# Attention and MLP-mixer kernel: keys in three chunks of 128 rows and a block-diagonal remainder, one score group a pair, PSUM tiles of two banks

## Chip, cores, metric

One core of one Trainium2 chip. The metric is the device time of one execution in microseconds (us), slowest (here: only) core, median of several runs. The kernel before takes 408.87 us (406.52 to 409.55).

The kernels of each comparison ran on the same chip as the kernel before. All medians below are of such runs. Different experiments ran on different chips, so across experiments the ratios compare better than the medians. A ratio is the mean time of one kernel's fast runs over the mean of the kernel before's fast runs of the same rounds, so it is not quite the ratio of the medians beside it. Times inside a profile are from the start of the profiled span.

## The reference

```python
# q, k, v: (8 batches, 12 heads, 448 rows, 64), tau = 0.1
q_n = q / (norm(q) + 1e-6);  k_n = k / (norm(k) + 1e-6)
attn = softmax(q_n @ k_n^T / tau)                    # per head
x    = (attn @ v) with heads side by side            # (8, 448, 768)
h    = relu(x^T @ w_tok1) @ w_tok2                   # over the 448 rows, 256 wide
u    = x + h^T
out  = u + relu(u @ w_ch1) @ w_ch2                   # over 768 columns, 1536 wide
```

## The kernel before

It works on pairs of heads: 6 pairs a batch, 48 in all. For a pair: load q, k, v (sync queue); square and sum them; scale q and k by their norms on POOL (`kq`); transpose (`qk`, by PE at first, by a DMA transpose from pair 12 on); scores on PE (`psS`), exp on ACT (`pt`), P times V (`psO`), divide (`x`), the two token matmuls (`psR`, `rt`, `psU`), the sum `u`, and a DMA transpose of `u` (`ut`), which the channel MLP (`psG`, `psF`) reads when all six pairs of the batch are there. MLP units (one `psG` or `psF` of six or twelve matmuls) are fed between the steps of later pairs, so that PE need not wait.

```python
# 4 chunks of SC = 112 rows; ps: 4 one-bank PSUM tiles, ps2: 2 two-bank tiles
def load_v(i):                                    # load_qk is the same for q and k
    ...
    nc.sync.dma_start(out=pipe[i]["v"][:].rearrange("p g c e -> p g (c e)"),
                      in_=v[b, h0:h0 + 2].rearrange("g (p c) e -> p g (c e)", c=NCH))
def tpose_dma(i):                                 # needs kq of pair i, from POOL
    ...
    nc.sync.dma_start_transpose(out=st["qk"]..., in_=st["kqn"]...)
def tok2(i, pe=False):
    ...                                           # psU, then u = psU + x
    nc.sync.dma_start_transpose(out=ut[b][:, pj], in_=u.rearrange("p m d -> p (m d)"))

for i in ...:                                     # one pair; cut to its order
    if pj == 0 and b >= 2:
        queue += ch2_units(b - 2)
    score(i, 0); score(i, 1)
    sums(i + 4); ...; squares(i + 5)
    feed(quota * 0.22)
    pv(i - 1, 0); pv(i - 1, 1)
    scaled(i + 2); tpose_dma(i + 2)
    cast_v(i); load_v(i + 4)
    feed(quota * 0.28, least)
    score(i, 2); score(i, 3)
    feed(quota * 0.25, least)
    tok1(i - 1)
    feed(quota * 0.25, least)
    tok2(i - 1)                                   # same pair as tok1
    if pj == 0:
        queue += ch1_units(b - 1)                 # behind ch2 units that are still queued
```

Of the kernel before, what the change touches and what calls it, by code (L numbers as in the profile page):

```python
# [7 lines left out]
FP32 = mybir.dt.float32  # L8
# [14 lines left out]
def kernel(  # L23
# [35 lines left out]

    MAIN = [(128 * m, 128 * (m + 1)) for m in range(3)]  # L60
# [21 lines left out]
    ps = ctx.enter_context(tc.tile_pool(name="ps", bufs=4, space=bass.MemoryType.PSUM))  # L82
    ps2 = ctx.enter_context(tc.tile_pool(name="ps2", bufs=2, space=bass.MemoryType.PSUM))
# [10 lines left out]

    def load_qk(i):
        b, h0 = i // NPAIR, 2 * (i % NPAIR)
        if i // HP not in half:
            n = i // HP
            half[n] = dict(ssq=nrm.tile([SC, 2, 6 * NCH], FP32, name=f"ssq_{n}", tag="ssq"),
                           rn=nrm.tile([SC, 2, 6 * NCH], FP32, name=f"rn_{n}", tag="rn"))  # L100
        st = pipe[i] = {}
        for nm, src in (("q", q), ("k", k)):
            st[nm] = qkv.tile([SC, 2, NCH, E], FP32, name=f"{nm}f_{i}", tag=f"{nm}f")
            nc.sync.dma_start(out=st[nm][:].rearrange("p g c e -> p g (c e)"),
                              in_=src[b, h0:h0 + 2].rearrange("g (p c) e -> p g (c e)", c=NCH))

    def load_v(i):
        b, h0 = i // NPAIR, 2 * (i % NPAIR)
        pipe[i]["v"] = qkv.tile([SC, 2, NCH, E], FP32, name=f"vf_{i}", tag="vf", bufs=4)
        nc.sync.dma_start(out=pipe[i]["v"][:].rearrange("p g c e -> p g (c e)"),  # L110
                          in_=v[b, h0:h0 + 2].rearrange("g (p c) e -> p g (c e)", c=NCH))
# [6 lines left out]
    tiny = cst.tile([SC, 1], FP32, name="tiny")  # L118
    nc.gpsimd.memset(tiny[:], 1e-18)
    eps = cst.tile([SC, 1], FP32, name="eps")  # L120
# [10 lines left out]
    for i in range(NV):  # L131
        vt = cst.tile([SC, 6, NCH, E + 2], FP16, name=f"vt{i}")
        nc.gpsimd.memset(vt[:, :, :, E:E + 2].rearrange("p g c e -> p (g c) e"), 1.0)
        vts.append(vt)
    pts = []
    for i in range(2):
        pt = cst.tile([SC, 8 * S + 64], FP16, name=f"pt{i}")
        nc.gpsimd.memset(pt[:, 8 * S:8 * S + 64], 0.0)
        pts.append(pt)
    nc.gpsimd.memset(w1t[64:128, 3, :], 0.0)  # L140
# [33 lines left out]
    def cast_v(i, eng=None):  # L174
        g = 2 * (i % HP)
        (eng or nc.gpsimd).tensor_copy(
            out=vts[(i // HP) % NV][:, g:g + 2, :, 0:E].rearrange("p g c e -> p (g c) e"),
            in_=pipe[i]["v"][:].rearrange("p g c e -> p (g c) e"))

    def square(i, a, act=False):  # L180
        if "sq" not in pipe[i]:
            pipe[i]["sq"] = nrm.tile([SC, 2, 2 * NCH, E], FP32, name=f"sq_{i}", tag="sq")
        src = side(i, a).rearrange("p g c e -> p (g c) e")
        if act:
            nc.scalar.activation(out=pipe[i]["sq"][:, a], in_=src, func=AF.Square)  # L185
        else:
            nc.gpsimd.tensor_mul(out=pipe[i]["sq"][:, a], in0=src, in1=src)  # L187

    def side(i, a):
        return pipe[i]["kq"[a]][:]  # L190
# [5 lines left out]
    def sums(i, a0=0, a1=2):  # L196
        lo = 2 * NCH * (i % HP)
        nc.vector.tensor_reduce(out=half[i // HP]["ssq"][:, a0:a1, lo:lo + 2 * NCH],  # L198
                                in_=pipe[i]["sq"][:, a0:a1], axis=AXX.X, op=ALU.add)

    def norms(i0, i1, a0=0, a1=2, dve=False, act=False):
        n = i0 // HP
        sl = slice(2 * NCH * (i0 - HP * n), 2 * NCH * (i1 - HP * n))
        ssq, rn = half[n]["ssq"][:, a0:a1, sl], half[n]["rn"][:, a0:a1, sl]
# [10 lines left out]
    def scale(i, a, eng=None):  # L215
        st = pipe[i]
        if "kqn" not in st:
            st["kqn"] = att.tile([SC, 2, NCH, 2, E], FP16, name=f"kq_{i}", tag="kq")
        lo = 2 * NCH * (i % HP)
        rn = half[i // HP]["rn"][:, a, lo:lo + 2 * NCH].rearrange("p (g c) -> p g c", g=2)  # L220
        (eng or nc.gpsimd).tensor_tensor(out=st["kqn"][:, a].rearrange("p c g e -> p g c e"), in0=side(i, a),  # L221
                                         in1=_bcast_free(rn, E), op=ALU.mult)
# [5 lines left out]
    def tpose(i, a0=0, a1=2):  # L228
        st = pipe[i]
        if "qk" not in st:  # L230
            st["qk"] = att.tile([128, 2, NCH, SC], FP16, name=f"qk_{i}", tag="qk")
        pst = ps.tile([128, a1 - a0, NCH, SC], FP16, name=f"pst_{i}_{a0}", tag="b")
        for a in range(a0, a1):
            for c in range(NCH):
                nc.tensor.transpose(pst[:, a - a0, c, :], st["kqn"][:, a, c].rearrange("p g e -> p (g e)"),  # L235
                                    id16[:SC, :SC])
        nc.vector.tensor_copy(out=st["qk"][:, a0:a1], in_=pst[:])

    def tpose_dma(i):
        st = pipe[i]  # L240
        st["qk"] = att.tile([128, 2, NCH, SC], FP16, name=f"qk_{i}", tag="qk")
        nc.sync.dma_start_transpose(out=st["qk"][:].rearrange("p a c s -> p (a c) s"),
                                    in_=st["kqn"][:].rearrange("p a c g e -> p (a c g e)"))

    def warm(n):
        if "warm" not in pipe:
            pipe["warm"] = ps.tile([128, 128], FP32, name="warm", tag="b")
        for _ in range(n):
            nc.tensor.matmul(pipe["warm"][:], id16[:], id16[:], start=True, stop=True)

    def score(i, c):
        qk = pipe[i]["qk"][:].rearrange("p a c s -> p (a c s)")
        psS = ps2.tile([128, 2, 512], FP32, name=f"psS_{i}_{c}", tag="s")
        for hh in range(2):
            hb = hh * 64
            nc.tensor.matmul(psS[:, hh, 0:S], qk[hb:hb + 64, c * SC:c * SC + 128],  # L256
                             qk[hb:hb + 64, S:2 * S], start=True, stop=True)
        nc.scalar.activation(out=pts[i % 2][:, 2 * S * c:2 * S * (c + 1)].rearrange("p (h s) -> p h s", h=2),  # L258
                             in_=psS[0:SC, :, 0:S], func=AF.Exp, scale=inv_tau)

    def pv(i, hh):
        st = pipe[i]
        b = i // NPAIR
        if hh == 0:
            st["x"] = att.tile([128, 4, 128], FP16, name=f"x_{i}", tag="x", bufs=3)
        vt = vts[(i // HP) % NV]
        g = 2 * (i % HP) + hh
        psO = ps.tile([128, 4, E + 2], FP32, name=f"psO_{i}_{hh}", tag="b")
        for m, lo in enumerate(windows(b)):
            for c in range(NCH):  # L270
                at = (2 * c + hh) * S + lo
                nc.tensor.matmul(psO[:, m, 0:E + 1], pts[i % 2][:, at:at + 128],  # L272
                                 vt[:, g, c, 0:E + 1], start=(c == 0), stop=(c == NCH - 1))
# [5 lines left out]
    def tok1(i):  # L279
        st = pipe[i]  # L280
        w1 = (0, 1, 2, 3) if (i // NPAIR) % 2 == 0 else (4, 0, 1, 2)
        psR = ps.tile([128, TT, 128], FP32, name=f"psR_{i}", tag="b")
# [7 lines left out]
    def tok2(i, pe=False):  # L290
# [5 lines left out]
        psU = ps.tile([128, 4, 128], FP32, name=f"psU_{i}", tag="b")  # L296
# [17 lines left out]
    def m_ch1(b, ct):  # L314
# [4 lines left out]
        psG = ps.tile([128, S], FP32, name=f"psG_{b}_{ct}", tag="b")  # L319
        for dt in range(DT):  # L320
            nc.tensor.matmul(psG[:], wc1t[:, dt, ct * 128:(ct + 1) * 128],  # L321
# [275 lines left out]
```

## Time and profile before

| | before |
|---|---|
| profiled span, mean clock | 406.0 us, 0.982 |
| first score of pair 7 / 12 / 14 / 47 | 50.0 / 80.5 / 98.7 / 343.6 us |
| pairs 14 to 47 (33 pairs) | 244.9 us, with 372 `psG` and 444 `psF` matmuls |
| from pair 47's first score to the end | 62.4 us |

I split the span like this throughout: the start up to pair 14, the steady part, and the end.

```profile
143.44 1.20 SPq L305 DMA_TRANSPOSE ut<-u  x1
144.69 0.58 SPq L104 DMA_DIRECT2D qf<-in_q_dram  x1
145.32 0.45 SPq L104 DMA_DIRECT2D kf<-in_k_dram  x1
145.88 1.22 SPq L242 DMA_TRANSPOSE qk<-kq  x1
147.20 0.59 SPq L110 DMA_DIRECT2D vf<-in_v_dram  x1
```

There are five issues a pair. The `ut` transpose stands where `u` has just been made, with nothing in front of it that waits for POOL.

### The profile page before, as it was taken

The page shows a single profiled execution, that of the slowest core. Times are in us where ns is not written, and L with a number is a line of the kernel's source. Part 1 is how long each engine was busy: PE and PEld are TensorE (multiplying, and loading weights), DVE is VectorE, ACT ScalarE, POOL GpSimd, SP SyncE. Part 2 cuts the span into 40 slices and gives each one's busy share as a digit, 9 for nine tenths or more (in the row PEclk, how much of TensorE's full clock was granted, in tenths as well). Part 3 has the DMA queues.
Part 4 walks back from the last instruction along what each step waited for, and adds up shares of the span by engine and source line. Part 5 has one row for each costly group of instructions (what it writes and reads, how often), then busy time and mean ns, then how long its engine had stood idle before and what let it go on. Part 6 is the DMA issues. An engine that isn't in the chain of part 4 may idle for free.

```text
span 406.0 us, 10118 instructions
## 1 busy us (share of the span) xinstructions
PE 389.1 (96%) x4146; PEld 240.4 (59%) x4146; DVE 206.4 (51%) x441; ACT 240.8 (59%) x392; POOL 218.5 (54%) x257
## 2 busy tenths in 40 slices
PE   6978799999999999999999999999999999999995
PEld 5656566566555665656656655556655666655562
DVE  5767877655454466554555555635636345312031
ACT  5857789954676438773587437773588535521400
POOL 7797999948557480949175852949092800000000
PEclk9868999999999999999999999999999999999999
DMA  8999999978859786867759697978974433103022
GB/s 198 239 175 251 246 262 230 209 195 180 201 142 191 140 200 157 197 161 171 201 127 187 156 184 188 164 152 187 195 130 94 114 81 92 28 15 116 2 74 81
DMA packets 102590, 64.07 MB, mean 158 GB/s; under 512 B 61328, under 2 KB 98960, under 8 KB 102544
## 3 DMA queue, kind: packets, MB, share of 16 engines
q1 hardware_dynamic: 96928, 58.22, 64.0%
q0 software_dynamic: 5616, 5.21, 8.1%
q8 instruction: 32, 0.52, 0.6%
q14 instruction: 14, 0.11, 0.1%
HBM read 43.45 MB, written 11.01 MB: 134 GB/s over the span
## 4 chain that ended last, share of the span: by engine, by line
PE 87%; DMA 5%; DVE 4%; POOL 1%; issue 1%; ACT 1%; SPq 0%; DVEq 0%; POOLq 0%
PE psF L336 27%; PE psG L321 27%; PE psO L272 12%; PE psS L256 10%; PE psU L299 5%; PE psR L285 5%; DMA kf<-in_k_dram 4%; DVE ssq L198 2%; DMA qf<-in_q_dram 1%; DVE x L276 1%; PE pst L235 1%; POOL kq L221 0%; ACT sq L185 0%; DVE ost L340 0%; DVE rt L288 0%
## 5 line engine op out<-in xcount | busy, mean ns | idle before, releaser
L258 ACT ACTIVATE pt<-psS 112x896 f16<-112x896 f32 x192 | 166.2, 914 | 84.4 <-PE psS L256 84.1
L321 PE MATMUL psG<-ut,wc1t 128*128 128x448 f16 x576 | 122.4, 353 | 0.0
L336 PE MATMUL psF<-wc2t,gt 128*128 128x384 f16 x672 | 116.6, 326 | 0.0
L221 POOL TENSOR_TENSOR kq<-kf,rn 112x512 f16<-112x512 f32 x47 | 50.0, 1063 | 99.3 <-ACT rn L213 86.3
L336 PEld LDWEIGHTS <-gt 128*128 128x128 f16 x672 | 63.1, 98 | 43.4 <-issue 5.2
L340 DVE TENSOR_TENSOR ost<-psF,u 128x384 f32<-128x384 f32 (+1 forms) x64 | 35.7, 557 | 96.2 <-PE psF L336 96.0
L324 ACT ACTIVATE gt<-psG 128x448 f16<-128x448 f32 x96 | 52.3, 545 | 53.7 <-PE psG L321 53.5
L321 PEld LDWEIGHTS <-wc1t 128*128 128x128 f16 x576 | 51.3, 98 | 46.6 <-issue 8.2
L198 DVE TENSOR_REDUCE ssq<-sq 112x16 f32<-112x1024 f32 (+1 forms) x49 | 58.1, 1189 | 9.0 <-ACT sq L185 6.4
L272 PEld LDWEIGHTS <-pt 112*128 112x128 f16 x1536 | 53.5, 99 | 15.5 <-ACT gt L324 7.0
L256 PE MATMUL psS<-qk 64*128 64x448 f16 x384 | 56.2, 363 | 3.5 <-ACT pt L258 2.7
L272 PE MATMUL psO<-vt,pt 112*128 112x65 f16 x1536 | 59.3, 195 | 0.1
L302 DVE TENSOR_TENSOR u<-psU,x 128x512 f16<-128x512 f32 x48 | 33.1, 689 | 34.2 <-PE psU L299 34.2
L187 POOL TENSOR_TENSOR sq<-kf 112x512 f32<-112x512 f32 x46 | 47.7, 1037 | 3.9 <-DMA kf<-in_k_dram 3.4
L221 POOL TENSOR_TENSOR kq<-qf,rn 112x512 f16<-112x512 f32 x45 | 46.8, 1041 | 0.0
L288 DVE TENSOR_SCALAR rt<-psR 128x256 f16<-128x256 f32 x48 | 20.2, 421 | 46.8 <-PE psR L285 46.6
L276 DVE TENSOR_TENSOR x<-psO,rec 128x256 f16<-128x256 f32 x96 | 40.8, 425 | 3.3
L187 POOL TENSOR_TENSOR sq<-qf 112x512 f32<-112x512 f32 x39 | 40.5, 1037 | 0.0
L285 PE MATMUL psR<-x,w1t 128*128 128x128 f16 x384 | 29.8, 221 | 2.6 <-DVE x L276 2.6
L285 PEld LDWEIGHTS <-w1t 128*128 128x128 f16 x384 | 25.0, 99 | 11.6 <-issue 3.3
L299 PEld LDWEIGHTS <-w2t 128*128 128x128 f16 x384 | 25.9, 100 | 9.0 <-issue 2.1
L299 PE MATMUL psU<-rt,w2t 128*128 128x128 f16 x384 | 30.1, 223 | 0.4 <-DVE rt L288 0.2
(40 smaller groups left out, 156.0 us busy)
## 6 DMA issues: line engine op xcount, KB each, us to landing
qf<-in_q_dram SPq DMA_DIRECT2D x48, 224.0 KB, 3.8
kf<-in_k_dram SPq DMA_DIRECT2D x48, 224.0 KB, 3.7
vf<-in_v_dram SPq DMA_DIRECT2D x48, 224.0 KB, 3.7
out_dram<-ost SPq DMA_DIRECT2D x8, 336.0 KB, 3.1
wc1t<-in_moe_w_ch_dram POOLq DMA_DIRECT2D x4, 576.0 KB, 8.2
wc2t<-in_moe_w_ch_dram POOLq DMA_DIRECT2D x2, 1152.0 KB, 16.3
out_dram<-ost SPq DMA_DIRECT2D x8, 288.0 KB, 2.9
out_dram<-ost SPq DMA_DIRECT2D x8, 240.0 KB, 2.8
```

Of the source, the lines that this page charges most:

```text
L187: nc.gpsimd.tensor_mul(out=pipe[i]["sq"][:, a], in0=src, in1=src)
L198: nc.vector.tensor_reduce(out=half[i // HP]["ssq"][:, a0:a1, lo:lo + 2 * NCH], in_=pipe[i]["sq"][:, a0:a1], axis=AXX.X, op=ALU.add)
L221: (eng or nc.gpsimd).tensor_tensor(out=st["kqn"][:, a].rearrange("p c g e -> p g c e"), in0=side(i, a), in1=_bcast_free(rn, E), op=ALU.mult)
L256: nc.tensor.matmul(psS[:, hh, 0:S], qk[hb:hb + 64, c * SC:c * SC + 128], qk[hb:hb + 64, S:2 * S], start=True, stop=True)
L258: nc.scalar.activation(out=pts[i % 2][:, 2 * S * c:2 * S * (c + 1)].rearrange("p (h s) -> p h s", h=2), in_=psS[0:SC, :, 0:S], func=AF.Exp ...
L272: nc.tensor.matmul(psO[:, m, 0:E + 1], pts[i % 2][:, at:at + 128], vt[:, g, c, 0:E + 1], start=(c == 0), stop=(c == NCH - 1))
L276: nc.vector.tensor_tensor(out=st["x"][:, :, hh * E:(hh + 1) * E], in0=psO[:, :, 0:E], in1=_bcast_free(rec[:], E), op=ALU.mult)
L285: nc.tensor.matmul(psR[:, tt], w1t[:, w1[m], tt * 128:(tt + 1) * 128], st["x"][:, m], start=(m == 0), stop=(m == 3))
L299: nc.tensor.matmul(psU[:, m], w2t[:, tt, lo:lo + 128], st["rt"][:, tt], start=(tt == 0), stop=(tt == TT - 1))
L321: nc.tensor.matmul(psG[:], wc1t[:, dt, ct * 128:(ct + 1) * 128], ut[b][:, dt].rearrange("p m s -> p (m s)")[:, lo:lo + S], start=(dt == 0) ...
L324: nc.scalar.activation(out=gt[:, ct, (b % 2) * S:(b % 2 + 1) * S], in_=psG[:], func=AF.Relu)
L336: nc.tensor.matmul(psF[:], gt[:, ct, lo:lo + 128], wc2t[:, ct, dh * DH:(dh + 1) * DH], start=(ct == 0), stop=(ct == CT - 1))
```

## The change

Its intent: fewer switches of PE's tiling mode, fewer and fuller score matmuls. The keys of a head come in three chunks of 128 rows. The last 64 keys of both heads share a fourth chunk, with block-diagonal zeros, so that one 128-row matmul scores both heads (`score_rest`). Their P times V part runs directly behind the score group in the same 64-row mode (`pv_rest`). PSUM becomes three two-bank and two one-bank tiles. The core of the diff (cut: tile shapes, memsets, the first six pairs, weight padding, MLP functions that only gain a `wide` argument):

```diff
-    ps = ...(tc.tile_pool(name="ps", bufs=4, ...))
-    ps2 = ...(tc.tile_pool(name="ps2", bufs=2, ...))
+    ps = ...(tc.tile_pool(name="ps", bufs=2, ...))
+    ps2 = ...(tc.tile_pool(name="ps2", bufs=3, ...))
+    def load_rows(t, src):                       # for k and v
+        nc.sync.dma_start(out=t[:, 0:2 * KC]..., in_=src[:, 0:128 * KC]...)
+        nc.sync.dma_start(out=t[:, 2 * KC], in_=src[:, 128 * KC:S])
     def scale(i, a, eng=None):
+        ...                                      # 3 chunks of k in one instruction, and
+        if a == 0:
+            for g in range(2):
+                p = slice(64 * g, 64 * g + 64)
+                (eng or nc.gpsimd).tensor_scalar_mul(out=kq[p, 0, KC, g], in0=src[p, 2 * KC], scalar1=rn[p, 2 * KC:KS])
+    def score_rest(i):
+        psQ = ps2.tile([128, 512], FP32, ...)
+        nc.tensor.matmul(psQ[:, 0:S], qk[:, 0, KC], qk[:, 1, :, 0:SC], start=True, stop=True)
+        nc.scalar.activation(out=pts[i % 3][...], in_=psQ[:, 0:S], func=AF.Exp, scale=inv_tau)
+    def pv_rest(i):                              # 8 matmuls of 64 rows, two banks in turn
+        ...
+    def refill(b, n):
+        while queue:
+            unit()
+        queue.extend(ch1_units(b) + ch2_units(b))
+        fed[:] = [0.0, sum(t for t, _ in queue) / n]
-    (the order of the kernel before, above)
+    for i in range(NPAIR + 1, NP_ALL):
+        for c in range(KC):
+            score(i, c)
+        pv_rest(i - 1); pv(i - 1, 0); pv(i - 1, 1)
+        if pj == 2 and b > 1:
+            refill(b - 1, 6)                     # batch b-1's MLP starts at once
+        side(i)                                  # load_qk, sums, squares, scaled,
+                                                 # tpose_dma(i + 2), cast_v(i), load_v(i + 4)
+        unit(True)
+        score_rest(i)
+        tok2(i - 2)                              # a pair later than tok1(i - 2)
+        ...                                      # units that are due
+        tok1(i - 1)
```

## The prediction

> **What bounds the kernel now.** I read the page first, busy times and slices:
>
> ```profile
> PE 389.1 (96%) x4146; PEld 240.4 (59%) x4146; DVE 206.4 (51%) x441; ACT 240.8 (59%) x392; POOL 218.5 (54%) x257
> ...
> PE   6978799999999999999999999999999999999995
> ...
> PEclk9868999999999999999999999999999999999999
> DMA  8999999978859786867759697978974433103022
> ```
>
> PE is full from slice 6 (about 52 us) to the end, at full clock; only the first eighth has PE gaps and a reduced clock (6 in slice 3). The DMA row is highest in just that part (8 and 9). The chain that ended last agrees: PE 87%, DMA 5%. Next, how full PE is when it is full, by stretches (us, PE, PEld, DVE, ACT, POOL busy, clock, DMA share, GB/s):
>
> ```profile
> 20.00:30.00 10.00, 7.60 (x92) 5.64 (x90) 6.79 (x13) 6.34 (x11) 9.80 (x12) 0.64 1.02 174
> ...
> 80.00:320.00 240.00, 239.89 (x2630) 144.91 (x2629) 125.61 (x266) 152.29 (x238) 145.74 (x161) 1.00 0.76 167
> ```
>
> From 80 to 320 us no other engine is over 64%, so there time is the sum of PE's work. The same stretch holds 1056 matmuls of psO, 32 a pair of heads: 33 pairs, 240/33 = 7.27 us a pair. "PE busy" says nothing of how well it is used, so I read the timeline of one pair (start, length of what is merged):
>
> ```profile
> 201.94 0.55 PE L256 MATMUL psS<-qk 64*128 64x448 f16 x4
> 202.42 1.19 PE L272 MATMUL psO<-vt,pt 112*128 112x65 f16 x32
> 203.45 1.30 PE L321 MATMUL psG<-ut,wc1t 128*128 128x448 f16 x6
> 204.68 0.55 PE L256 MATMUL psS<-qk 64*128 64x448 f16 x4
> ```
>
> Starts, not lengths, add up here. Six psG matmuls take 6 x 0.189 = 1.13 us (starts inside a group are 0.189 us apart; 448 columns take 0.187 at the 2.4 GHz of the clock-gate page named below), so psG's share ends at 204.58, psS starts 0.10 later, and the next psG at 205.16. A score group of four thus takes 0.58 us. In the instruction records its matmuls start 3 ns apart in pairs and the pairs 0.20 apart: the two heads' 64-row matmuls run side by side. Two pairs need 0.374 us of columns; 0.207 is lost on entering and leaving. All 79 groups between 52 and 340 us show it (median 0.581). psO: 203.45 - 202.42 = 1.03 us for 32 matmuls, 32 ns each.
>
> **What the Trainium skill says.** "TensorEngine Tiling (Array Packing)", Key Properties: going from one tiling mode to another drains the array. The trace agrees and gives the size, 0.10 us in and 0.10 us out. "TensorE: Matmul & The Clock Gate", Part 3, The mechanism: matmuls on different row groups overlap, some 4 ns apart; here 3 ns. The same page, Part 1: after an idle window the clock is halved until work has been dense again; the 0.64 in 20 to 30 us agrees. "DMA: Bandwidth & Descriptors", Why a DMA increments its semaphore by 16 and not by 1 (How many engines): a transfer runs on the largest number up to 16 that divides the slowest dimension of both sides. All loads before have 112 partitions outside, so 16; nothing in this trace shows a smaller number.
>
> **The change, part by part.**
>
> *PE, score.* Before, a pair has two groups of two side-by-side pairs: 2 x 0.581 = 1.162 us. After, one group of three (3 x 0.19 + 0.207 = 0.78) and one 128-row matmul for both heads' last 64 keys (0.189, no mode change because of block-diagonal zeros): 0.97. Columns are the same (4 x 448 either way); what is saved is one entry and exit, 0.2 us.
>
> *PE, P times V.* Before 32 x 32 ns = 1.03 us. After 24 x 32 ns = 0.77 and eight 64-row matmuls that sit directly behind the score group, in its mode, alternating row halves and PSUM banks. If each two run side by side as the scores do: 4 x about 0.035 = 0.14 (estimate); if not, 8 x 32 ns and nothing is saved. Saving 0.11, or 0.
>
> Together 0.31 us a pair (0.2 without overlap). Pairs 7 to 47 run where PE is full: 41 x 0.31 = 12.7 us (8.4). The other matmuls do not change.
>
> *ACT.* Four exps of 896 columns at 914 ns = 3.66 us a pair become three and one of 448. The relu of 128x448 has a row, 545 ns, so 3.29 us: 0.37 less. That is beside PE's work in the full stretch and worth something only before 52 us, where `psS` waits for `pt` (2.7 us in five waits): up to 7 x 0.37 = 2.6 us.
>
> *POOL.* The k scaling shrinks from 512 to 384 columns (1063 to about 800 ns) but gains two 64-column pieces of about 0.2 us; the k square and v cast shrink by an eighth (0.13, 0.08 us). Even, and POOL is at 61%. *DVE:* the reduction has 960 columns for 1024 (1210 to about 1135 ns); eleven memsets at the start fit before its first work at 4.4 us.
>
> *PSUM and order.* psO and what else is narrow now share two banks, where four served. `pv_rest` needs both, directly after the scores, and one was just filled by psR, whose relu takes 421 ns on DVE. The score group lasts 0.78 us, so this mostly fits, but when DVE is inside a reduction PE waits: I allow 0.07 us a pair, 3 us. Third two-bank tile: scores no longer wait for two exps. tok2 now follows a whole pair later, so its waits on `rt` stay away.
>
> *DMA.* q loads stay: 224 packets of 1024 B. k and v become 256 packets of 768 B and 128 of 256 B, and three more matters follow. The transposes go from 112 to 128 rows (896 to 1024 packets each). In the packet records 1024 B takes a median 46 ns, 256 B 18, 3072 B 121, so 768 B should take about 37 (interpolated). Spread over 16 engines a pair costs 42 x 46 = 1.93 us of each engine before, and 14 x 46 + 32 x 37 + 16 x 18 = 2.12 after: +10%, harmless. But the small load has two heads outside on the DRAM side and 128 partitions on the other, and by the rule above it runs on two engines: 64 packets each. For those two the pair costs 14 x 46 + 32 x 37 + 128 x 18 = 4.13 us, twice as much. With transposes (64 + 32 packets, 1.73), stores (0.57) and the rest they are busy about 6.6 us of a pair of 7.0: only just under the bound. Before 52 us the pairs follow every 4.6 us (first `psS` after a wait at 34.25, then 38.85) and the weights pass too, so there these two engines are over it. Loads up to k of pair 10 and v of pair 7 need 11 x 2.41 + 8 x 1.77 = 41 us there, with weights and transposes (about 11 us by the same packet times) 52 us, against the 50 us at which pair 7 starts now. I expect the start to lengthen by 5 to 9 us if the rule holds (I give it two chances in three), 2 us if not; against it stand the exps' 2.6 us and about 1 us from the extra warming matmuls, which keep the clock from the 0.64.
>
> Sum: 408.9 - 12.7 (PE) + 3 (PSUM waits) + 2 (start: 0.67 x 7 + 0.33 x 2 - 3.6 = 1.7) + 1 (later waits for two full DMA engines, a third of a possible 3) = about 402 us.
>
> **Rivals.**
> 1. *The PE saving arrives whole and the small loads spread or hide.* For: the full stretch has no engine over 64%, loads run seven pairs ahead, mean DMA share is 0.76 with peaks above. Then 409 - 12.7 - 2 + 2 = 396, or 393 if no PSUM wait appears.
> 2. *Two DMA engines become the bound.* For: the share of 0.76 to 1.2 is already high, the chain before 60 us holds waits for kf and qf, and 6.6 of 7.0 us leaves no room for HBM packets of 256 B slower than the 18 ns, which I know only from transposes inside SBUF. At 25 ns it is 7.5 us a pair: 41 x (7.5 - 6.96) = +22 us on rival 1, about 418. Against: a schedule this tuned would hardly keep it.
> 3. *The PV remainder does not overlap,* or its weight loads do not: 4 us less gain, about 406.
> 4. *PSUM with two narrow banks stalls PE.* At 0.3 us a pair all is given back: 409. Against: between the users of one bank lies at least one MLP unit of 1.13 us, longer than any evacuation (reciprocal and multiply 0.6, u 0.69).
>
> **Range and chances.** The PE term is the firmest (8 to 14 us off); the DMA terms can cost nothing or 20 us. 391 covers rival 1 with full overlap and a better start; 416 covers rival 2 at its milder end. The 2% line, 400.7 us, lies just under the point, so faster and same are about even; slower needs rival 2.
>
> **What would show it.** Right: score matmuls in groups of six, 0.58 for two groups gone; per pair 7.0 us between 80 and 320; remainder matmuls 3 ns apart in pairs; small loads landing later than large ones; pair 7 starting at 50 to 57 us. Wrong: PE idle or half clock after 80 us with the releaser DMA or POOL (rival 2), psO waiting for DVE `rt` (rival 4), remainder starts 32 ns apart (rival 3), or a start shorter than 48 us.

## More of the kernel before

The loads of q, k and v, the stores and the DMA transposes are issued by one engine, SP, in program order (the weights by POOL). The rows with SPq are the sync queue's timeline in the steady part (start, length of the issue, what is issued).

The group rows of POOL, the engine that prepares k and q (count, busy us and mean ns of one, then idle time before them):

```profile
L221 POOL TENSOR_TENSOR kq<-kf,rn 112x512 f16<-112x512 f32 x47 | 50.0, 1063 | 99.3 <-ACT rn L213 86.3
L187 POOL TENSOR_TENSOR sq<-kf 112x512 f32<-112x512 f32 x46 | 47.7, 1037 | 3.9 <-DMA kf<-in_k_dram 3.4
```

From 49 to 83 us POOL has hardly a gap, and waits for k loads take only 3.4 us in all.

## The result

The changed kernel takes 453.54 us (453.34 to 453.63, four runs), the kernel before 409.21 (406.52 to 410.17) in the same rounds: ratio 1.109, 95% interval 1.104 to 1.115. It is slower by 44 us and far outside the range of 391 to 416. The page of the changed kernel, parts 1, 2 and 4:

```profile
PE 395.9 (88%) x4120; PEld 255.8 (57%) x4120; DVE 212.5 (47%) x454; ACT 224.3 (50%) x392; POOL 243.7 (54%) x352
...
PE   6878599779599996999699997999599997999995
PEclk9889779989799998999889998999899996999999
...
PE 67%; DMA 8%; DVE 8%; POOL 7%; ACT 4%; issue 3%; SPq 1%; POOLq 0%; ACTq 0%
```

The PE row is no longer a row of nines. From slice 8 on it falls to 5, 6 or 7 every few slices, down to the end, and the clock row falls to 6, 7 or 8 about there. The chain holds PE for 67% and not 87%; DMA, DVE and POOL have 8, 8 and 7%.

| us | before | changed |
|---|---|---|
| start, to pair 14 | 98.7 | 113.5 |
| pairs 14 to 47 | 244.9 | 284.3 |
| rest | 62.4 | 54.1 |
| span | 406.0 | 451.9 |

The rest is shorter because the changed kernel has done more of the MLP by pair 47 (426 `psG` and 432 `psF` matmuls between 14 and 47, against 372 and 444). At 0.19 and 0.163 us each that is 54 x 0.19 - 12 x 0.163 = 8.3 us. For the same work the steady part is thus 284.3 - 8.3 - 244.9 = 31 us longer. The start is 14.8 us longer; it holds 12 `psF` matmuls more (72 against 60), so for the same work 14.8 - 12 x 0.163 = 12.8.

**PE's work did get shorter.** One pair of the changed kernel on PE, to hold against the four lines of before in the prediction:

```profile
106.86 0.74 PE L275 MATMUL psS<-qk 64*128 64x448 f16 x6
107.44 0.30 PE L295 MATMUL psO<-vt,pt 64*128 64x65 f16 x8
107.67 0.92 PE L304 MATMUL psO<-vt,pt 128*128 128x65 f16 x24
108.43 2.11 PE L368 MATMUL psF<-wc2t,gt 128*128 128x384 f16 x12
110.38 0.35 PE L282 MATMUL psQ<-qk 128*128 128x448 f16 x1
110.57 0.61 PE L331 MATMUL psU<-rt,w2t 128*128 128x128 f16 x8
```

By starts: six score matmuls 0.58 us, the eight remainder matmuls 0.23 (with one mode switch), P times V 0.76, the 128-row score 0.19 (110.57 - 110.38). With about 0.1 to enter the mode (as before) that is 1.86 us, against 2 x 0.58 + 1.03 = 2.19 before. The overlap is there: 0.23 less the switch of 0.10 leaves 0.13 us for eight matmuls, not 8 x 0.032. In the instruction records the eight start within 92 to 111 ns in every pair from 14 to 46, where 32 ns apart would take 224; 72 of the 132 couples start less than 10 ns apart, as the prediction had asked for.

**Where PE stands instead.** Two waits of PE that the kernel before does not have (us in total, times, longest):

```profile
PE psG L353 <- DMA ut<-u: 21.3, 6, 4.5
PE psO L295 <- POOL vt L198: 11.8, 10, 4.0
```

and the sync queue's waits for POOL and for `u` in the changed kernel, then the one for POOL before:

```profile
SPq L262 <- POOL vt L198: 46.1, 10, 9.5
SPq L337 <- DVE u L334: 27.0, 8, 6.6
```
```profile
SPq L242 <- POOL vt L176: 31.6, 15, 3.4
```

Six times, once a batch, the first `psG` of a batch waits for the last `ut`. SP waits 46 us for POOL in front of the `qk` transposes. It waited there before too, but shorter at a time and with no `ut` transpose behind it that was urgent. The timeline around the first of the six, all engines, lines left out:

```profile
111.22 0.69 DVE L334 TENSOR_TENSOR u<-psU,x 128x512 f16<-128x512 f32 x1
...
112.64 0.54 SPq L113 DMA_DIRECT2D qf<-in_q_dram  x1
...
113.79 1.04 POOL L236 TENSOR_TENSOR kq<-qf,rn 112x512 f16<-112x512 f32 x1
...
114.86 1.76 SPq L262 DMA_TRANSPOSE qk<-kq  x1
...
116.37 1.11 PE L353 MATMUL psG<-ut,wc1t 128*128 128x448 f16 x5
116.72 0.52 SPq L101 DMA_DIRECT2D vf<-in_v_dram  x1
117.96 2.04 SPq L337 DMA_TRANSPOSE ut<-u  x1
...
121.95 0.53 PE L353 MATMUL psG<-ut,wc1t 128*128 128x448 f16 x1 [4.47 <-DMA ut<-u]
122.28 0.58 PE L282 MATMUL psQ<-qk 128*128 128x448 f16 x1
122.65 1.06 PE L331 MATMUL psU<-rt,w2t 128*128 128x128 f16 x8
```

`u` is done at 111.91. Its transpose is issued at 117.96, because the queue in front of it holds the pair's loads, the `qk` transpose (which waits until POOL has scaled q, 113.79 plus 1.04) and the v loads. `psG` has started at 116.37 with the five pairs that are there, needs the sixth, and PE stands for 4.47 us. After that PE runs at half clock: the next matmul of 448 columns takes 0.37 us to its successor and not 0.19, eight `psU` matmuls take 1.06 and not 0.61. The records show the same doubled spacing after each of the six stalls.

Two things of the change make this. The instruction records of the last pair of each batch (six batches, the first and the last left out) show both, in us:

| | `u` done to its transpose issued | `u` done to the first `psG` of the batch |
|---|---|---|
| before | 0.0 to 0.4 | 12.2 to 28.4 |
| changed | 4.9 to 6.1 | 3.9 to 4.5 |

Before, ch1 units joined the queue behind ch2 units, so a transpose had at least 12 us. Now `refill` starts them at once, and `tok2`, a pair later and behind `side`, gets its place in the queue last.

### The profile page after: what moved, and what is told of

Its sections match the earlier page's. It is cut to its first block, busy times and chain, and to the rows that moved or that the text cites. A ratio compares the mean times of both kernels' runs of the same rounds, so it can differ in the third digit from the quotient of the medians.

```text
span 451.9 us, 10222 instructions
## 1 busy us (share of the span) xinstructions
PE 395.9 (88%) x4120; PEld 255.8 (57%) x4120; DVE 212.5 (47%) x454; ACT 224.3 (50%) x392; POOL 243.7 (54%) x352
## 4 chain that ended last, share of the span: by engine, by line
PE 67%; DMA 8%; DVE 8%; POOL 7%; ACT 4%; issue 3%; SPq 1%; POOLq 0%; ACTq 0%
PE psG L353 22%; PE psF L368 20%; PE psO L304 7%; PE psS L275 6%; PE psU L331 5%; DMA ut<-u 5%; DMA kf<-in_k_dram 4%; PE psR L317 3%; POOL kq L236 3%; DVE ssq L215 3%; DVE x L308 2%; POOL kq L243 2%; PE psO L295 2%; PE psQ L282 2%; POOL sq L208 1%
## 5 line engine op out<-in xcount | busy, mean ns | idle before, releaser
L276 ACT ACTIVATE pt<-psS 128x896 f16<-128x896 f32 x144 | 122.3, 917 | 71.1 <-PE psS L275 71.1
L353 PE MATMUL psG<-ut,wc1t 128*128 128x448 f16 x576 | 127.5, 372 | 21.5 <-DMA ut<-u 21.3
L236 POOL TENSOR_TENSOR kq<-kf,rn 128x384 f16<-128x384 f32 x47 | 39.9, 849 | 106.7 <-ACT rn L229 105.9
L353 PEld LDWEIGHTS <-wc1t 128*128 128x128 f16 x576 | 56.5, 103 | 50.7 <-issue 11.0
L215 DVE TENSOR_REDUCE ssq<-sq 128x15 f32<-128x960 f32 (+2 forms) x49 | 54.9, 1124 | 6.6 <-POOL sq L208 5.1
L208 POOL TENSOR_TENSOR sq<-kf 128x448 f32<-128x448 f32 x46 | 42.9, 932 | 19.6 <-DMA kf<-in_k_dram 12.1
L304 PE MATMUL psO<-vt,pt 128*128 128x65 f16 x1152 | 46.0, 197 | 0.0
L243 POOL TENSOR_SCALAR kq<-kf,rn 64x64 f16<-64x64 f32 x94 | 41.4, 440 | 4.2
L304 PEld LDWEIGHTS <-pt 128*128 128x128 f16 x1152 | 40.0, 99 | 2.7
L307 DVE RECIPROCAL rec<-psO 128x4 f32<-128x4 f32 x96 | 17.0, 177 | 51.1 <-PE psO L304 51.1
L275 PE MATMUL psS<-qk 64*128 64x448 f16 x288 | 38.3, 369 | 1.8 <-DVE ost L372 0.9
```

Of the source, the lines that this page charges most:

```text
L208: nc.gpsimd.tensor_mul(out=dst, in0=src, in1=src)
L215: nc.vector.tensor_reduce(out=half[i // HP]["ssq"][:, i % HP, sl], in_=sqs[i % 3][:, sl], axis=AXX.X, op=ALU.add)
L236: (eng or nc.gpsimd).tensor_tensor(out=kq[0:NP[a], a, 0:n].rearrange("p c g e -> p g c e"), in0=src[:, 0:2 * n].rearrange("p (g c) e -> p ...
L243: (eng or nc.gpsimd).tensor_scalar_mul(out=kq[p, 0, KC, g], in0=src[p, 2 * KC], scalar1=rn[p, 2 * KC:KS])
L275: nc.tensor.matmul(psS[:, hh, 0:S], qk[hb, 0, c], qk[hb, 1, :, 0:SC], start=True, stop=True)
L276: nc.scalar.activation(out=pts[i % 3][:, 2 * S * c:2 * S * (c + 1)].rearrange("p (h s) -> p h s", h=2), in_=psS[:, :, 0:S], func=AF.Exp, s ...
```

## The experiments

The theories. A: the small loads run on two engines and these are the bound (the prediction's second rival). B: the order on the sync queue. C: POOL has more to do, and casts v last. All kernels gave correct results.

**1. Small loads over 16 engines (e1), the order (e2), both (e3).** e1 splits each small load by head:

```diff
-        nc.sync.dma_start(out=t[:, 2 * KC], in_=src[:, 128 * KC:S])
+        for g in range(2):
+            nc.sync.dma_start(out=t[64 * g:64 * g + 64, 2 * KC], in_=src[g, 128 * KC:S])
```

e2 leaves all work the same and issues a pair's loads and `qk` transpose after `tok2`:

```diff
-    load_qk(i + 7); ...; tpose_dma(i + 2); ...; load_v(i + 4)     # in side(i)
+    later = [load_qk(i + 7), ..., tpose_dma(i + 2), load_v(i + 4)]
     ...
     tok2(i - 2)
+    for f in later: f()
```

> The changed kernel with each small load (32 KB, 64 rows of each head) issued as two loads of 64 partitions, one a head, so that the slowest dimension is 64 and 16 engines share it; nothing else differs. Theory A (two DMA engines are the bound): the small loads cost the start (pair 12 begins 19.7 us later than in the kernel before) and make the transposes late, so the start comes back to within 3 us of before and the total falls from 453.5 to 425-430; to 400-410 if the six waits of psG for the transposed ut (21 us) vanish with it. Theory B (order on the sync queue): the waits for ut come from transposes queued behind work that waits for POOL, so they stay at 3 to 4.5 us each and the total stays at 445 or above. DMA packets of 4 B rise from 5984 to 8,8xx if the loads now use 16 engines each.

> The changed kernel with small loads as they are, but in the main loop the sync queue's loads and the qk transpose of an iteration are issued after tok2, so the ut transpose no longer stands behind the v load and the qk transpose, which wait for POOL. Theory B: each of the six waits for ut (3 to 4.5 us, and the half clock after it) vanishes, 25 to 35 us less, about 420-428. Theory A: the transposes are slow because two engines are full, whatever the order, and the total stays above 445.

> Both edits. If A and B each hold for their own share (start, waits for ut), the gains add: 453.5 - 25 - 30 = about 398-402, what the prediction's PE term alone gives (396 to 402). If only one is real, no better than the better of the two.

Measured: e1 462.81 us (1.130), e2 420.84 (1.028), e3 430.65 (1.052). e2 takes away 32.7 of the 44.3 us, with every byte and every instruction kept. Pairs 14 to 47 go from 284.3 to 249.7 us and the wait of `psG` for `ut` is gone. In the same records as above, `u` waits 0.0 to 1.7 us for the issue. The same place in e2, lines left out:

```profile
110.63 0.69 DVE L334 TENSOR_TENSOR u<-psU,x 128x512 f16<-128x512 f32 x1
...
112.97 1.25 SPq L337 DMA_TRANSPOSE ut<-u  x1
114.28 0.57 SPq L113 DMA_DIRECT2D qf<-in_q_dram  x1
...
115.78 1.34 PE L353 MATMUL psG<-ut,wc1t 128*128 128x448 f16 x6
```

The `ut` transpose now goes out ahead of the loads, and six `psG` matmuls run without a gap. e1 makes it worse: two more issues a pair stand in front of the same transposes. Its wait of `psG` for `ut`, which was 21.3 us:

```profile
PE psG L354 <- DMA ut<-u: 31.0, 6, 6.7
```

But in e1 pair 7 starts at 52.7 and not 56.4 us. So B is the main cause, and A is worth something in the start only. In e3 `psS` waits for `qk`, 10.0 us in ten waits, and `psG` for `ut` again, 7.0 in five: with two issues more a pair the sync queue seems too full in the steady part as well.

**2. Parts of C and of the start, each on top of e2.** e6: `cast_v(i)` first in `side`, not last. e7: the two 64 x 64 pieces of the k scaling by ACT from pair 8 on. e9: small loads split as in e1 for the first 14 pairs alone. e8: all three.

```diff
 def side(i):                                   # e6
+    cast_v(i)
     ...
-    cast_v(i)
 for g in range(2):                             # e7, in scale()
+    if i >= 8:
+        nc.scalar.activation(out=kq[p, 0, KC, g], in_=src[p, 2 * KC], func=AF.Copy, scale=rn[p, 2 * KC:KS])
+        continue
```

> e2_order (420.8 us) with one more move: the v cast is the first POOL work of an iteration instead of the last. In e2_order between pairs 14 and 47 the scores' successor psO waits eleven times, 10.5 us in all, eight of them for the POOL cast, which stands behind the scaling that waits for ACT's norms; in pair 11 another 4.4 us. Theory C (POOL order, new because psO now follows the scores directly): these waits go, 8 to 13 us less, 408-413. Rival (the waits are PSUM, or POOL is simply full): less than 3 us.

> e2_order with the two small pieces of the k scaling (64x64, 440 ns each on POOL where I had estimated 200) on ACT from pair 8 on. If POOL's load is what delays the cast, POOL loses 0.9 us a pair and the same waits shrink: 4 to 10 us less. If only the order matters (theory C), under 3 us; ACT, at half load, gains about 0.5 us a pair and may delay an exp.

> e2_order with the small loads of the first 14 pairs split so that 16 engines share them, the later ones left on two. Theory A cut down to the start: in e2_order pair 7 starts at 58.9 us and its chain holds one wait of 13.5 us for a k load; with the split it starts at about 53 as in e3_both, and the total falls by 4 to 8 us, 413-417, without the cost of the 28 further loads a batch that made e3_both slower. If the start is bound by something else: no change in total.

> All of it: sync order, cast first, small pieces on ACT from pair 8, split small loads in the first 14 pairs. If the three causes add: 420.8 - 10 - 6 - 3 = about 400-404, 1.5 to 2.5% under the kernel before. If POOL or the start only hides another wait: 405 or more.

Measured: e6 417.07 (1.017), e7 423.21 (1.025), e9 416.06 (1.016), e8 415.67 (1.014). Two of e7's four runs, the profiled one among them, fell in the slow state; the ratio is of the two fast ones (417.69 and 422.26), and its profile is not used. e6 gains 3.8 us: the waits of `psO` for `vt` in the steady part are gone, and pairs 14 to 47 take 244.3 us. With the 8.3 us of additional MLP work that is 8.9 us less than before for the same work, 0.27 us a pair. e9 gains 4.8, in the start (pair 14 at 108.4 instead of 113.2). e7 gains nothing that its runs can show, and e8 less than e6 and e9 together would; in it PE's transposes wait 8.4 us for the pieces on ACT.

**3. The two-engine loads by themselves (e4, e5).** The kernel before, with two more loads a pair that nobody reads, of the same size and number of packets, once with two heads outside and once with 128 rows outside:

```diff
 # in load_qk with src = k, and in load_v with src = v
+    t = qkv.tile([128, E], FP32, ...)
+    nc.sync.dma_start(out=t[:], in_=src[b, h0:h0 + 2, 384:S])      # e4
+    nc.sync.dma_start(out=t[:], in_=src[b, h0, 0:128])             # e5
```

> The kernel before with two extra loads a pair whose result nobody reads: the last 64 key (value) rows of both heads into a tile of 128 partitions, two heads outside, as in the changed kernel: 128 packets of 256 B each, on two engines if the factor rule holds. It is the cost of such loads alone, on top of all bytes of before. If two engines full of small packets bound the changed kernel (the prediction's second rival), this costs at least 15 us: 425 or more. If they cost only in the start, as the split in the changed kernel suggests, 5 to 10 us: 414 to 419, all of it before 60 us of the span. 4 B packets: 5792 + 192 = 5984 if on two engines.

> The control of e4_two: the same number of extra loads, packets and bytes, but from one head's first 128 rows, so that 128 is outside on both sides and all 16 engines take part. If it is the two engines that cost in e4_two, this is within 2 us of the kernel before (409 to 411); if bytes, packets or the issues on the sync queue cost, it is like e4_two. 4 B packets rise by 96 x 16 = 1536, to 7328.

Measured: e4 433.81 (1.059), e5 416.15 (1.016), before 409.60. The packets of 4 bytes on the hardware queue (their numbers fit one for each engine that takes part in a transfer) are 5792 before, 5984 in e4 (96 x 2 more), 7328 in e5 (96 x 16 more). The changed kernel has 5984 too. So the small loads do run on two engines, and that alone costs 17.7 us against the same bytes over 16; bytes and issues cost 6.6. Both costs lie before pair 14, which starts at 98.7, 107.3 (e5) and 125.0 us (e4). From there to pair 47 all three take 244.9 us. POOL's wait for k, e4 and then e5 (before it was 3.4):

```profile
POOL sq L194 <- DMA kf<-in_k_dram: 39.6, 17, 5.4
```
```profile
POOL sq L194 <- DMA kf<-in_k_dram: 19.8, 11, 5.9
```

What goes with it on the sync queue of the changed kernel:

```profile
65.62 4.40 SPq L103 DMA_DIRECT2D vf<-in_v_dram  x1
70.12 7.13 SPq L113 DMA_DIRECT2D qf<-in_q_dram  x1
```

The issue of a small v load lasts 4.40 us instead of some 0.55, and the next, a q load, 7.13. For 12 us SP gets hardly anything out. Summed over the first 100 us, the issues last 54.7 us before, 69.4 in e5, 94.1 in e4 and 94.1 in the changed kernel, 76.1 when its small loads are split (e1). That two-engine loads lengthen the issues is shown by e4 against e5; how they do it is not. What SP issues late, the `qk` transposes and POOL get late.

**4. The best mixture (e10), and the pieces on DVE (e11).** e10 is e2 with e6's cast and e9's split. e11 in addition runs the 64 x 64 pieces on DVE behind `tok2`'s add, from pair 12 on.

> The three cures that each gained something, together and without the ACT pieces that gained nothing: loads and qk transposes issued after tok2, the v cast first on POOL, the small loads of the first 14 pairs split over 16 engines. Measured singly on top of the reordering (420.8 us): the cast -3.8, the split -4.8. If the two act in different places (cast: the waits of psO for vt from pair 14 on; split: the first 10 pairs) they add: about 412 us, 1.007 of the kernel before; pair 7 at about 53, pair 14 at about 108, and 240 to 246 us from pair 14 to pair 47. If the cast already removed what the split removes (the stall at pair 11), about 416.

> As e10_mix, but the two 64 by 64 pieces of the k scaling run on DVE (behind tok2's add, before the transpose that needs them) from pair 12 on, which takes 0.88 us a pair from POOL. If POOL's load is what still holds the start back around pairs 10 to 12 and makes transposes late, the stall at pair 11 shrinks from about 12 us to 7 or less and the time falls by 3 to 5 us against e10_mix, to about 407, the level of the kernel before. If POOL is no longer on the path there, the time stays within 1 us of e10_mix; if DVE's in-order queue now holds up relu and adds, psS and psU waits for DVE grow and it is slower.

Measured: e10 409.99 (0.9998, 0.993 to 1.007), e11 418.72 (1.022). e10 is level with the kernel before; its steady part is 243.8 us, its start 111.2. The cast first, which ends the waits of the steady part, costs some 3 us in the start both times that it was added (pair 14 at 116.8 in e6 against 113.2 in e2, at 111.2 in e10 against 108.4 in e9): `psS` of pair 12 then waits 5.7 us for `qk` in e10, 2.0 in e9. The cast first from pair 14 on alone was not tried. e11 loses 8.7 us, and the reason is a surprise. The two groups of the piece, by engine (count, busy us and mean ns, idle before):

```profile
L252 DVE TENSOR_SCALAR kq<-kf,rn 64x64 f16<-64x64 f32 x72 | 59.4, 825 | 4.2 <-ACT rn L233 3.6
L252 POOL TENSOR_SCALAR kq<-kf,rn 64x64 f16<-64x64 f32 x24 | 10.7, 444 | 1.1
```

A stretch of its timeline, first DVE, then POOL:

```profile
155.31 1.90 DVE L252 TENSOR_SCALAR kq<-kf,rn 64x64 f16<-64x64 f32 x2
```
```profile
155.62 1.04 POOL L240 TENSOR_TENSOR kq<-qf,rn 112x512 f16<-112x512 f32 x1
156.61 0.56 POOL L202 CAST vt<-vf 128x448 f16<-128x448 f32 x1
```

The same piece has a mean of 825 ns on DVE and 444 on POOL. The two DVE pieces end at 157.21, when POOL's cast has just ended (157.17). 20 of the 72 took 234 to 256 ns. The other 52 took 351 ns to 3.29 us, and each of them ended within 60 ns after the end of a POOL instruction. "SBUF — State Buffer", Who interferes with whom, in the Trainium skill says that DVE and POOL share a pair of ports, that `tensor_scalar` can take it, and that the later one waits for the whole instruction. The trace agrees.

**5. What is left in the start (e12, e14 to e18).** e12: e10 with the v loads from pair 5 on issued by ACT, and one more buffer for them. e14: e12 with all small loads split. e15: as e12, but only the v loads of pairs 12 to 16. e16: e15 with the `qk` transposes of pairs up to 13 ahead of the loads of that turn. e17: e10 with only that. e18: e17 with the second channel weights requested a pair earlier.

```diff
-    load_rows(pipe[i]["v"], v[...], i, nc.sync)
+    load_rows(pipe[i]["v"], v[...], i, nc.scalar if i > 4 else nc.sync)            # e12, e14
+    load_rows(pipe[i]["v"], v[...], i, nc.scalar if 12 <= i < 17 else nc.sync)     # e15, e16
-    later.append(tpose_dma(t))
+    later.insert(0, tpose_dma(t))                                                  # e16, e17, e18
-    if i == 8: weights_ch2()
+    if i == 7: weights_ch2()                                                       # e18
```

> As e10_mix, but the v loads from pair 5 on are issued by the ACT queue (with one more vf buffer), not by the sync queue. In the profile of e10_mix the sync queue spends 84 of the first 100 us issuing (before: 55), and the qk transpose of pair 12, whose input POOL finished at 82.6 us, is issued at 91.75; the stall at pair 11 to 12 (12.7 us against 6.3 before) waits for it. If the issue time on the sync queue is what holds the start back, that transpose is issued within 3 us of its input, the stall shrinks to 8 us or less, pair 14 starts at 104 to 107 instead of 111, and the time is 403 to 406, better than both kernels. If POOL, which is full from 53 to 87 us and has 0.7 us more work a pair than before, paces the start, pair 14 starts at 110 or later and the time stays at 409 to 411. If the issues cost ACT's exps their place, psO or psS waits grow and it is slower than e10_mix.

> As e12_vact, with the small k and v loads split over 16 engines for all pairs, not for the first 14 alone. With the v loads off the sync queue its four extra issues a pair no longer overload it (in e3_both they cost 10 us in waits of psS for qk). If the two-engine loads still cost something after pair 14, this is 1 to 3 us below e12_vact; if they are hidden there, as pairs 14 to 47 of e10_mix (243.8 us against 244.9 before) suggest, it is within 1.5 us of it, or slower for the extra issues.

> As e10_mix, with the v loads of pairs 12 to 16 alone (issued in pairs 8 to 12) on the ACT queue. e12_vact lost 11 us before pair 7, where the exps on ACT stood behind its loads, but took 30.2 us from pair 8 to 12 where e10_mix takes 33.4. If that difference was the sync queue's backlog, this keeps e10_mix's first eight pairs (pair 8 at about 62) and gains about 3 to 6 us after: pair 14 at 105 to 108, about 404 to 407 us. If e12_vact was faster there only because everything came later and DMA and POOL had caught up, it stays at 409 to 411.

> As e15_vact_few, and in the pairs up to 11 the qk transposes are issued ahead of the loads of that pair (behind tok2 still), as the transpose of pair 12 had its input 9 us before its issue in e10_mix. It moves that issue forward by about 1.9 us: 1 to 2 us below e15_vact_few if the stall at pair 11 to 12 still ends with that transpose, within 1 us of it if not.

> As e10_mix, with only the qk transposes of the pairs up to 11 ahead of the loads of that pair. Alone it is worth at most the 1.9 us of the loads that stood before it: 407.5 to 410, pair 12 at 93 to 95.

> As e17_first, with the 2.3 MB of the second channel weights requested in pair 7 and not in pair 8, some 5 us earlier. In e10_mix the DMA share is 0.57 and 0.76 in the stretches 55 to 60 and 60 to 65 us and 1.15 to 1.25 from 65 to 80, where a v load's issue takes 5.1 us on the sync queue. If that crowding of loads and weights is what makes the transposes late, the work moves into the dip, no issue takes over 3 us, pair 14 starts at 103 to 107 (108.1 in e17_first) and the time is 404 to 408, level with or better than the kernel before. If the weights do not matter for it, 409 to 411 as e17_first; if they now stand before the k loads of pairs 13 and 14, up to 414.

Measured: e12 420.25 (1.023; one of its four runs was slow), e14 421.04 (1.028), e15 418.42 (1.021), e16 418.39 (1.021), e17 410.75 (1.004), e18 412.53 (1.008, five rounds). None beats the kernel before. Moving v to ACT's queue does not help, because ACT then stands in front of these loads. Timeline of e15 on ACT:

```profile
67.26 0.54 ACT L287 ACTIVATE pt<-psQ 128x448 f16<-128x448 f32 x1
79.71 0.43 ACTq L101 DMA_DIRECT2D vf<-in_v_dram  x1
...
82.18 0.98 ACT L360 ACTIVATE gt<-psG 128x448 f16<-128x448 f32 x2 [14.38 <-DMA ut<-u]
```

Between an exp that ends at 67.80 and the next relu ACT stands for 14.38 us. The profile names `ut` as the releaser, only because it came last: the relu reads `psG`, which was long done. What ACT stood at is the v load at the head of its program. The instruction records tell what that load waited for. In these programs all loads, stores and transposes that SP and ACT issue take eight completion semaphores in turn, whichever of the two issues them, and an issue waits until the transfer that had its semaphore before, eight issues ago, has landed. ACT's load at 79.71 waited for a q load that the sync queue had issued at 67.15 and whose parts landed from 78.8 us on. "DMA: Bandwidth & Descriptors", Issuing engines are not separate DMA queues, says that transfers run on the same 16 engines whoever starts them; the run agrees in that moving the issues brought nothing (e12, e15), and adds that in these programs they even share the eight semaphores.

e14 against e12 (fast runs: 421.2 against 419.3 us on average, ranges overlapping) shows no cost of two-engine loads after pair 14. e17 moves pair 14 from 111.2 to 108.1 us and the time not at all. In e18 no issue lasts over 2.4 us any more, but POOL now runs dry at 70 to 75 us (1.09 of 5 us busy), and pair 14 is at 110.8.

One table puts these together: when POOL has scaled pair 14, and what it did until then (e19 follows below).

| kernel | done at (us) | POOL busy | POOL idle |
|---|---|---|---|
| before | 82.7 | 72.2 | 10.5 |
| before + 16-engine loads (e5) | 91.0 | 72.2 | 18.9 |
| before + two-engine loads (e4) | 110.1 | 71.9 | 38.2 |
| changed | 102.9 | 79.8 | 23.1 |
| e10 | 98.9 | 80.5 | 18.4 |
| e8 (e10 with the pieces on ACT) | 97.0 | 74.3 | 22.7 |
| e18 | 101.6 | 80.4 | 21.2 |
| e19 | 95.8 | 80.5 | 15.3 |

The changed kernel is later by 20.2 us on POOL: 7.6 of longer work and 12.6 of waiting, most of it for loads (waits for k 11.3 us against 3.0). Taking the pieces off POOL (e8) saved 6.2 us of work, and 4.3 of it came back as waiting. POOL alone does not set when pair 14 starts: it starts 16.0 us after POOL's end before, where PE is busy 47.3 of the 48.7 us from pair 7 to 14, and 10.6 (changed), 12.3 (e10), 9.2 (e18) and 8.6 us (e19) after it elsewhere.

**6. Fewer transfers (e19).** If eight transfers in flight are the limit, it is their number that counts, not their bytes. The kernel before has five issues a pair, so eight cover 1.6 pairs. The changed kernel has seven (1.1 pairs), e10 nine up to pair 13 (0.9). e19 is e10 with one q load for two pairs and one small load per half of the partitions for two pairs, from pair 8 on: 6.5 issues a pair, same bytes. Its tiles hold two pairs, so that there are buffers for eight pairs of q and k (seven before) and six of v (four).

```diff
+    # in load_qk, even i of 8 and more; tiles hold two pairs
+    nc.sync.dma_start(out=two["q"][:].rearrange("p j (g c) e -> p (j g) (c e)", g=2),
+                      in_=q[b, h0:h0 + 4].rearrange("g (p c) e -> p g (c e)", c=NCH))
     # in load_rows
+    for g in range(2):
+        nc.sync.dma_start(out=t[64 * g:64 * g + 64, :, 2 * KC],
+                          in_=src[:, 128 * KC:S].rearrange("(j g) p e -> g p j e", g=2)[g])
```

> As e10_mix, with fewer loads for the same bytes: from pair 8 on one q load serves two pairs, and one small k (v) load serves one half of the partitions for two pairs, over 16 engines always. That is 6.5 sync queue issues a pair where e10_mix has 9 (pairs up to 13) or 7. The traces show that the loads, stores and transposes of the sync queue take eight completion semaphores in turn, and that each issue waits until the transfer eight issues before it has landed. If this window of eight transfers is what starves the start (it covers 1.6 pairs before, 1.1 in the changed kernel, 0.9 in e10_mix up to pair 13), pair 14 starts at 102 to 107 instead of 111 and the time is 402 to 406, below both kernels. If the DMA engines' bytes or POOL's longer work set the start whatever the window, pair 14 stays at 109 to 112 and the time at 408 to 412.

Measured: 405.68 us (405.40 to 406.65), before 408.08 in the same rounds: ratio 0.9935, 0.989 to 0.998. It is the only version that is below both kernels, by 0.6%, so still "the same" at 2%. Pair 14 starts at 104.4 us, as expected; the steady part takes 245.6. POOL's work up to pair 14 is that of e10, only its waiting has shrunk, by 3.1 us. The issues' summed length hardly changed (83.9 us of the first 100 in e10, 82.7 in e19), so it is not their length that mattered. Against e10 (ratio 0.993 to 1.007, another chip) the intervals overlap.

The forecast came true, but the traces do not bear out its reason. From 20 to 100 us the sync queue's waits for the landing of a transfer come to 5.5 us in e10 and 6.2 in e19: they did not shrink. In the changed kernel no issue of this stretch starts less than 0.7 us after the landing, eight issues before, that it needs: there the window does not bind directly. What shrank are the waits of the loads of q, k and v for ACT, DVE or POOL, 9.1 us in e10 and 2.6 in e19 (3.5 before, 16.2 in the changed kernel). A load has to wait for these engines only until its buffer is free, so the additional buffers are the likelier cause. No run has more buffers with the same number of transfers.

## Why the prediction was wrong

**PE, scores and remainder: right.** Predicted were 0.31 us a pair, of which 0.11 hung on the overlap. The timeline gives 2.19 - 1.86 = 0.33 before new waits, the steady part of e6 0.27 net. Over the 33 steady pairs that is 8.9 us. Rival 3 (no overlap) is false. In the changed kernel's time none of it can be seen.

**ACT, DVE: right, and worth nothing.** The exps take 3 x 0.917 + 0.54 = 3.29 us a pair, as worked out, the reduction of 960 columns 1.144 us (1.135 predicted). The 2.6 us expected from it in the start did not come: the start waits for loads and POOL.

**POOL "even": wrong in size.** The pieces were put at about 0.2 us each. They take 0.44:

```profile
L243 POOL TENSOR_SCALAR kq<-kf,rn 64x64 f16<-64x64 f32 x94 | 41.4, 440 | 4.2
```

By starts, a pair is 0.81 + 1.05 (two pieces) + 1.0 + 0.9 + 1.0 + 0.51 = 5.27 us of POOL against 4.58 before. In the steady part POOL has room, in the start it has none: 7.6 us more work up to pair 14. The v cast, last on POOL, also cost 3.8 us (e6), a wait I had not listed.

**PSUM waits, 3 us: too large.** The sign asked for, `psO` waiting for `rt`, does not appear. From pair 7 on `psS` waits 0.9 us for `ost`, in three waits, and `psO` once 0.3. `psU` waits 3.5 us for `rt`, but all before 56 us, in the pairs whose two token matmuls still stand in one turn. Rival 4 is false.

**DMA in the start: the mechanism was right, the end point was not.** The small loads run on two engines (5984 packets of 4 bytes), and pair 7 starts at 56.4, inside the 50 to 57 that I gave. Splitting the loads takes back 3.7 of these 6.4 us (e1, 52.7), so only part of the hit is owed to the rule. And I counted the start as over at pair 7, where PE filled up before. The backlog runs on to pair 12, and pair 14 is 14.8 us late, 12.8 for the same work, where the sum has 2. "Later 1 us" was fair: nothing after pair 14 (e4, e14). As an explanation of the whole loss rival 2 is false: splitting the loads alone made the kernel slower (e1), and the long stalls are not on the two engines.

**The step that failed** is in "PSUM and order": "tok2 now follows a whole pair later, so its waits on `rt` stay away". In the main loop they do stay away; but I looked only at what `tok2` waits for, and not at what waits for `tok2`. Its last action is a DMA issue on an in-order queue, now behind issues that wait for POOL; and its reader, the next batch's MLP, had been moved forward by `refill` from 12 or more us to about 4. Six stalls of 3.2 to 4.5 us (21.3 in all), each with half clock after it, and the waits for `vt` make up the steady loss: 284.3 - 244.3 = 40 us between the changed kernel and e6, 34.6 of it by the order alone (e2). The sum of the prediction has no term for it. My list of what would show me wrong named a PE idle after 80 us with the releaser DMA, but as a sign of rival 2; it was the sign, and the cause was another.

**What stays open.** In the profiled runs e10 loses 12.5 us in the start, somewhat more than the 9.6 that it gains afterwards, and e19 still 5.7 (2.0 of each are the 12 additional `psF`). e19 gave back about half, by fewer transfers in flight, more buffers or loads that start earlier; these are not separated, and the waits speak for the buffers. From pair 7 to 14 e19 takes 49.3 us, e10 58.3 and the kernel before 48.7: nearly all that e19 still loses lies before pair 7 (55.1 against 50.0). POOL's longer work (8.3 us up to pair 14, the same in e10 and e19) may be part of it, but no run took it away without adding waits elsewhere (e8, e11). The eight semaphores do not explain the two long issues of 4.40 and 7.13 us: the semaphores that they reuse had come 1.7 and 5.5 us before. That the two engines' own queues were full there is the likely reading, not a shown one. And no run kept the changed order but gave the channel MLP its old slack, so what the early `refill` costs by itself is not measured.

## What to carry to other kernels

When a change moves a step later, list the readers of its output with their slack and the queue that its output goes through, not only its own waits. An in-order DMA queue is an engine: give every issue on it a length and a place, put an issue that waits for a slow engine behind those that are ready, and count transfers and buffers as well as bytes. Where several resources are near full in a stretch, curing one can come back as waiting for another (6.2 us of POOL work became 4.3 us of waits in e8).

## What the Trainium skill lacked or had wrong

- "DMA: Bandwidth & Descriptors", Issuing engines are not separate DMA queues, calls the time to initiate a DMA "usually small relative to the DMA itself". For one load at a time that holds (0.45 to 0.6 us, against 3.7 to landing in the kernel before). But here the sync queue's issues last 94.1 of the first 100 us; one of 0.55 us lasted 4.40 and the next 7.13. The page has a section on back-pressure between cores, and no word on an issue of a core's own load that takes this long. ACT's 14.38 us are another matter: its load waited for a completion semaphore that the program uses in turn.
- The same page, Why a DMA increments its semaphore by 16 and not by 1, gives the rule for the number of engines, and the runs confirm it (192 more packets of 4 bytes for 96 loads, 1536 for 16-engine ones). It has no cost: 17.7 us here for 96 loads of 32 KB, all in the start.
- "TensorEngine Tiling (Array Packing)", Key Properties, states that a mode switch drains the array, without a size. Here about 0.10 us each way.
- No page has the time of a small `tensor_scalar` on POOL. Here a `tensor_scalar` with a scalar for each partition takes 440 ns for 64 x 64 elements, more than half of the 849 ns that the `tensor_tensor` of 128 x 384 takes. That suggests a large fixed part, but it is another operation, and no run varies the size.
- "SBUF — State Buffer", Who interferes with whom, is right about the shared ports. The size here: a DVE instruction that took 234 to 256 ns in 20 of 72 cases took 825 on average and up to 3289 beside a busy POOL.
